# One unit boundary of a fused attention and gated-FFN kernel: scores and attention outputs gathered in one place each

## The chip, the cores and the metric

The kernel runs on one core of one Trainium2 chip. The metric is device time of one execution in microseconds (us). The kernel before took 254.5 us, the median of three runs (254.49, 254.50 and 255.01 us). Engines are called by the names of the profile: PE is the matrix engine and PEld its weight loads, DVE the vector engine, ACT the scalar engine, POOL the GpSimd engine, SP the engine that here only issues transfers.

## The reference, cut to what matters

Inputs are q, k, v of shape (4, 8, 768, 64), that is batch, heads, positions, head size, and four weight matrices. First comes an attention in which each position sees a band of its neighbours and one summary of each block of 32 positions:

```python
k_sum = k.reshape(B, H, nb, 32, D).max(axis=3)
v_sum = v.reshape(B, H, nb, 32, D).mean(axis=3)
scores_l = scale * q @ k.T            # kept only where |i - j| < 16
scores_s = scale * q @ k_sum.T + log(32)
a = softmax(concat[scores_l, scores_s])
x = a @ concat[v, v_sum]              # then (4*768, 512)
```

Then a gated feed-forward with a gated residual:

```python
ffn = (gelu(x @ w_gate) * (x @ w_val)) @ w_out
out = x + sigmoid(x @ w_res) * ffn
```

The model width is 512 (8 heads of 64), the inner width 1536, and there are 3072 rows of x.

## The kernel before, in words

The rows are cut into eight units of 384 positions (`TU`), two to a batch entry. A unit has three sub-blocks of 128 rows (`NSUB`), and its heads are handled as four pairs (`hp`). All matrix operands are bf16. The order of instructions on every engine is the order in which the code issues them (`tc.manual_schedule()`), so the order of the source lines is the order of each engine's queue. The framework adds the waits.

The work of a unit has two halves. In the first, for each of twelve columns of the inner width (`fo`), PE makes `g` and `vv` (line 451), ACT takes the Gelu of `g` (456), and DVE multiplies it by `vv` into `gvT` (457). In the second, the output half, PE makes the residual gate `r` (`res_step`, 492) and ACT its tanh into `th` (495); PE multiplies `gvT` by `w_out` into `f` (`ffn_step`, 502), twelve matmuls for each sub-block; and DVE combines `th`, `f` and x in two instructions (`end_step`, lines 508 and 511), after which SP sends 128 rows out.

Interleaved with the output half of unit u, the attention of unit u + 1 is made. Its steps are:

- **Scores.** PE multiplies keys by queries, 48 small matmuls (6 tiles x 2 heads x 4 pairs); ACT takes the exponential into `p_all`; DVE multiplies `p_all` by a mask. `s_step` does one pair (12 matmuls, one exponential of 768 columns or two of 384, one mask product). `s_all` (lines 343 to 373) does all four pairs packed into six PSUM banks of 512 columns: two tiles of the pool `ps_mm`, the two banks of `ps_s`, and the one tile each of `ps_t` and `ps_o`. It has five exponentials and six mask products of 512 columns.
- **Attention outputs.** PE multiplies `p_all` by the values into `ao`, 12 matmuls a pair; DVE divides by the sum, two instructions a pair (`av_end`, lines 429 and 431), into `xn`. `av_step` does one pair. `av_all` (375 to 398) does all four, with the `ao` tiles of pairs 0 and 1 in `ps_t` and `ps_o`, and of pairs 2 and 3 in `ps_s`.
- **Turning x.** The next first half needs x with its columns on the partitions (`xT`). From unit 2 on transfers do this (`xt_dma`). For unit 1 PE does it (`xt_step`, lines 433 to 438): three transposes into one PSUM tile and one copy out, on DVE unless ACT's copy is passed.

Three functions hold the three kinds of output half: `first_out` (unit 0's, which makes the attention of unit 1), `mid_out` (units 1 to 6) and `last_out`. `mid_out` uses `s_all` and `av_all`, one place each. `first_out` uses `s_step` and `av_step` in three or four places.

PSUM tiles are shared in turn. `ps_mm` has four banks, taken round by round by `g`, `vv`, `r`, `f` and by two of `s_all`'s tiles. `ps_t` and `ps_o` have one tile each, so whoever takes such a tile waits until the one before it was read. `w_out` arrives in three chunks of four `fo` (issued on line 213): chunk 1 serves `ffn_step(.., 0, 4)`, chunk 2 `(.., 4, 8)`, chunk 3 `(.., 8, 12)`.

Of the kernel before, what the change touches and what calls it, by code (L numbers as in the profile page):

```python
# [15 lines left out]
def kernel(  # L16
# [11 lines left out]
    nc = tc.nc  # L28
# [9 lines left out]
    FO = DFF // 128  # L38
# [4 lines left out]
    NSUB = TU // 128  # L43
# [16 lines left out]
    ps_o = ctx.enter_context(tc.tile_pool(name="ps_o", bufs=1, space=bass.MemoryType.PSUM))  # L60
    ps_t = ctx.enter_context(tc.tile_pool(name="ps_t", bufs=1, space=bass.MemoryType.PSUM))
# [77 lines left out]
    with tc.manual_schedule():  # L139
# [182 lines left out]
        def s_step(u, hp, st, banks=None, tiles=None):  # L322
            if tiles:
                s, banks = tiles, True
            elif banks:
                s = [p.tile([128, 512], F32, tag=tag, name="s") for p, tag in banks]
            else:
                s2 = ps_s.tile([128, 2, 512], F32, tag="s", name="s")
                s = [s2[:, hh] for hh in range(2)]
            s_mm(u, hp, [x[:, 0:TU] for x in s])  # L330
            P = p_all[:, :, hp * HT:(hp + 1) * HT]
            if banks:
                for hh in range(2):
                    nc.scalar.activation(P[:, hh].rearrange("p t q -> p (t q)"), s[hh][:, 0:TU], AF.Exp,
                                         scale=scale, bias=bias_t[:])
            else:
                nc.scalar.activation(P.rearrange("p a t q -> p a (t q)"), s2[:, :, 0:TU], AF.Exp,
                                     scale=scale, bias=bias_t[:])
            if u:
                nc.vector.tensor_mul(P, P, maskt.unsqueeze(1).unsqueeze(1).to_broadcast([128, 2, HT, QT]))  # L340
            st["P", hp] = P

        def s_all(u):
            b, half = u // 2, u % 2
            kw, qt = kW[b % 2], qT[b % 2]
            s2 = None
            for i in range(3):
                if i == 0:
                    s = [ps_mm.tile([128, 512], F32, tag="mm", name="s") for _ in range(2)]
                elif i == 1:  # L350
                    s2 = ps_s.tile([128, 2, 512], F32, tag="s", name="s")
                    s = [s2[:, hh] for hh in range(2)]
                else:
                    s = [p.tile([128, 512], F32, tag=tag, name="s") for p, tag in TO2]
                for j in range(8):
                    hp, t = divmod(8 * i + j, HT)
                    tt = half * HT + t
                    for hh in range(2):
                        ps = slice(hh * 64, hh * 64 + 64)
                        nc.tensor.matmul(s[hh][:, j * QT:(j + 1) * QT], kw[ps, tt, hp, :],  # L360
                                         qt[ps, tt // 2, hp, (tt % 2) * QT:(tt % 2 + 1) * QT],
                                         start=True, stop=True, skip_group_check=True)
                js = slice(8 * i, 8 * i + 8)
                m = maskt.unsqueeze(1).to_broadcast([128, 8, QT])
                for hh in range(1 if i == 1 else 2):
                    if i == 1:
                        nc.scalar.activation(p_all[:, :, js].rearrange("p a j q -> p a (j q)"), s2[:], AF.Exp,
                                             scale=scale, bias=bias_t[:])
                    else:
                        nc.scalar.activation(p_all[:, hh, js].rearrange("p j q -> p (j q)"), s[hh][:], AF.Exp,  # L370
                                             scale=scale, bias=bias_t[:])
                for hh in range(2):
                    nc.vector.tensor_mul(p_all[:, hh, js], p_all[:, hh, js], m)  # L373
# [27 lines left out]
        TO2 = ((ps_t, "t"), (ps_o, "ao"))  # L401

        def av_step(u, hp, st, pool=ps_o, tag="ao"):
            b, half = u // 2, u % 2
            P = st["P", hp]
            ao = pool.tile([128, NSUB, 2, D + 1], F32, tag=tag, name="ao")
            for sub in range(NSUB):
                for hh in range(2):
                    for e in range(2):
                        t = 2 * sub + e  # L410
                        nc.tensor.matmul(ao[64 * e:64 * e + 64, sub, hh, :], P[:, hh, t, :],
                                         vext[b % 2][:, half * HT + t, 2 * hp + hh, 0:D + 1],
                                         start=True, stop=True, skip_group_check=True)
            av_end(hp, st, ao)
# [12 lines left out]
        def av_end(hp, st, ao):  # L427
            rz = work.tile([128, NSUB, 2, 1], F32, tag="rz", name="rz")
            nc.vector.reciprocal(rz[:], ao[:, :, :, D:D + 1])  # L429
            xn = st["xn"][:, hp].rearrange("p s (h d) -> p s h d", d=D)  # L430
            nc.vector.tensor_mul(xn, ao[:, :, :, 0:D], rz.to_broadcast([128, NSUB, 2, D]))  # L431

        def xt_step(u, ko, st, pool, tag, copy=nc.vector.tensor_copy):
            xp = pool.tile([128, TU], BF16, tag=tag, name="xp")
            for sub in range(NSUB):
                nc.tensor.transpose(xp[:, sub * 128:(sub + 1) * 128],  # L436
                                    st["xn"][:, ko, sub, :], ident[:])
            copy(st["xT"][:, ko, :], xp[:])
# [5 lines left out]
        def new_unit():  # L444
            return {"xn": upool.tile([128, KO, NSUB, 128], BF16, tag="xn", name="xn"),
                    "xT": upool.tile([128, KO, TU], BF16, tag="xT", name="xT")}
# [12 lines left out]
        def mm_tile(name):  # L459
            return ps_mm.tile([128, 512], F32, tag="mm", name=name)  # L460
# [27 lines left out]
        def res_step(st, sub):  # L488
            ss = slice(sub * 128, (sub + 1) * 128)
            r = mm_tile("r")  # L490
            for ko in range(KO):
                nc.tensor.matmul(r[:], st["xT"][:, ko, ss], w_res[:, ko, :],  # L492
                                 start=(ko == 0), stop=(ko == KO - 1))
            st["th", sub] = work.tile([128, DM], F32, tag="th", name="th")
            nc.scalar.activation(st["th", sub][:], r[:], AF.Tanh, scale=0.5)  # L495

        def ffn_step(st, gvT, sub, lo, hi):
            ss = slice(sub * 128, (sub + 1) * 128)
            if lo == 0:
                st["f", sub] = mm_tile("f")  # L500
            for fo in range(lo, hi):
                nc.tensor.matmul(st["f", sub][:], gvT[:, fo, ss], w_out[:, fo, :],  # L502
                                 start=(fo == 0), stop=(fo == FO - 1), skip_group_check=True)
# [13 lines left out]
        def end_step(u, st, sub):  # L517
            end_part(u, st, sub, st["f", sub], slice(0, DM))
# [19 lines left out]
        tk, tq, ao = {}, {}, {}  # L538
# [11 lines left out]
        st = new_unit()  # L550
        gvT = upool.tile([128, FO, TU], BF16, tag="gvT", name="gvT")
# [91 lines left out]

        def first_out(u, st, gvT, nst):
            n = u + 1
            other = dict(pool=ps_t, tag="t")
            turn = dict(pool=ps_t, tag="t", copy=nc.scalar.copy)
            s_step(n, 0, nst)
            s_step(n, 1, nst, TO2)
            for sub in range(NSUB):  # L650
                res_step(st, sub)
            ffn_step(st, gvT, 0, 0, 4)
            av_step(n, 0, nst)
            av_step(n, 1, nst, **other)
            s_step(n, 2, nst)
            ffn_step(st, gvT, 1, 0, 4)
            ffn_step(st, gvT, 2, 0, 4)
            ffn_step(st, gvT, 0, 4, 8)
            xt_step(n, 0, nst, **turn)
            av_step(n, 2, nst)  # L660
            s_step(n, 3, nst)
            ffn_step(st, gvT, 1, 4, 8)
            ffn_step(st, gvT, 2, 4, 8)
            ffn_step(st, gvT, 0, 8, FO)
            xt_step(n, 1, nst, **turn)
            av_step(n, 3, nst)
            ffn_step(st, gvT, 1, 8, FO)
            xt_step(n, 2, nst, **turn)
            xt_step(n, 3, nst, ps_o, "ao")
            end_step(u, st, 0)  # L670
            ffn_step(st, gvT, 2, 8, FO)
            end_step(u, st, 1)
            end_step(u, st, 2)

        def mid_out(u, st, gvT, nst):
# [25 lines left out]
        for u in range(NU):  # L701
# [7 lines left out]
            if u:  # L709
                gvT = upool.tile([128, FO, TU], BF16, tag="gvT", name="gvT")  # L710
# [48 lines left out]
            else:  # L759
                nst = new_unit()  # L760
                (mid_out if u else first_out)(u, st, gvT, nst)
                st = nst
# [30 lines left out]
```

## Time and profile before

| what | value |
|---|---|
| median of three runs | 254.5 us |
| the profiled execution's own time | 255.01 us |
| its span from first to last instruction | 252.9 us |
| PE busy | 248.1 us, 98% of the span |
| PE weight loads busy | 139.5 us, 55% |
| DVE busy | 159.0 us, 63% |
| ACT busy | 127.9 us, 51% |
| POOL busy | 96.5 us, 38% |
| granted PE clock, mean | 0.998 |
| `f` matmuls, line 502 (128x512) | 276 records, 63.6 us |
| `r` matmuls, line 492 (128x512) | 96, 23.1 us |
| unit 0's output half on PE, first score matmul to the next unit's first `g` | 38.17 to 51.67 us |

The span is the time between the first and the last instruction of the program; the execution's own time, 2.1 us longer, takes in what lies around it. A matmul's record is longer than the time until the next one may start, since matmuls are pipelined; what a group of matmuls costs is therefore read from the start of the group to the start of the next group.

### The profile page before, as it was taken

The page shows a single profiled execution, that of the slowest core. Times are in us where ns is not written, and L with a number is a line of the kernel's source. Part 1 is how long each engine was busy: PE and PEld are TensorE (multiplying, and loading weights), DVE is VectorE, ACT ScalarE, POOL GpSimd, SP SyncE. Part 2 cuts the span into 40 slices and gives each one's busy share as a digit, 9 for nine tenths or more (in the row PEclk, how much of TensorE's full clock was granted, in tenths as well). Part 3 has the DMA queues.
Part 4 walks back from the last instruction along what each step waited for, and adds up shares of the span by engine and source line. Part 5 has one row for each costly group of instructions (what it writes and reads, how often), then busy time and mean ns, then how long its engine had stood idle before and what let it go on. Part 6 is the DMA issues. An engine that isn't in the chain of part 4 may idle for free.

```text
span 252.9 us, 5881 instructions
## 1 busy us (share of the span) xinstructions
PE 248.1 (98%) x2328; PEld 139.5 (55%) x2328; DVE 159.0 (63%) x376; ACT 127.9 (51%) x210; POOL 96.5 (38%) x128
## 2 busy tenths in 40 slices
PE   8999999999999999999999999999999999999994
PEld 2676565565654665446554665546554565456544
DVE  6995796398557544768557545758557545754424
ACT  8885458256582338254572338243572338243320
POOL 8885442360632881247332990247331000000000
PEclk9999999999999999999999999999999999999999
DMA  5999999999403999959903999769903600140003
GB/s 78 178 182 197 197 204 207 178 168 235 68 4 62 199 148 125 104 158 157 139 3 62 207 151 149 74 169 152 133 3 62 167 4 0 34 156 0 3 0 124
DMA packets 98106, 29.33 MB, mean 116 GB/s; under 512 B 83224, under 2 KB 94944, under 8 KB 97984
## 3 DMA queue, kind: packets, MB, share of 16 engines
q0 software_dynamic: 68352, 14.76, 67.0%
q1 hardware_dynamic: 29728, 14.21, 27.1%
q8 instruction: 18, 0.29, 0.5%
q14 instruction: 8, 0.07, 0.1%
HBM read 29.36 MB, written 6.29 MB: 141 GB/s over the span
## 4 chain that ended last, share of the span: by engine, by line
PE 93%; DVE 5%; issue 1%; DVEq 0%
PE g L451 25%; PE vv L451 24%; PE f L502 24%; PE r L492 8%; PE ao L390 2%; PE s L360 2%; PE vs L282 1%; PE tp L220 1%; PE ao L423 1%; PE vs L290 1%; PE s L317 1%; PE wp L534 1%; DVE ks L237 1%; DVE o L511 1%; PE xp L436 1%
## 5 line engine op out<-in xcount | busy, mean ns | idle before, releaser
L451 PE MATMUL g<-xT,w_gate 128*128 128x384 bf16 x380 | 78.0, 326 | 0.0
L451 PE MATMUL vv<-xT,w_val 128*128 128x384 bf16 x380 | 77.7, 326 | 0.0
L456 ACT ACTIVATE ge<-g 128x384 f32<-128x384 f32 x81 | 39.7, 490 | 61.0 <-DVE gvT L457 30.0
L457 DVE TENSOR_TENSOR gvT<-ge,vv 128x384 bf16<-128x384 f32 x81 | 44.3, 549 | 38.1 <-PE vv L451 34.0
L502 PE MATMUL f<-w_out,gvT 128*128 128x512 bf16 x276 | 63.6, 379 | 0.0
L451 PEld LDWEIGHTS <-w_gate 128*128 128x128 bf16 x384 | 37.1, 98 | 26.2 <-issue 1.4
L451 PEld LDWEIGHTS <-w_val 128*128 128x128 bf16 x384 | 37.6, 98 | 25.2 <-issue 0.5
L502 PEld LDWEIGHTS <-gvT 128*128 128x128 bf16 x276 | 26.2, 98 | 30.6
L107 POOL DMA_DIRECT2D vext<-in_v_dram x32 | 24.1, 767 | 15.2 <-DMA w_out<-in_moe_w_out_dram 5.6
L495 ACT ACTIVATE th<-r 128x512 f32<-128x512 f32 x24 | 13.6, 614 | 30.8 <-PE r L492 30.8
L508 DVE SCALAR_TENSOR_TENSOR th<-th,f 128x512 f32<-128x512 f32 (+2 forms) x26 | 16.6, 640 | 13.4 <-PE f L502 13.4
L492 PE MATMUL r<-w_res,xT 128*128 128x512 bf16 x96 | 23.1, 380 | 0.0
L302 POOL COPY vext<-vsum 32x1536 bf16<-32x1536 bf16 x12 | 17.2, 1463 | 11.8 <-DMA vsum<-vpart 11.6
L373 DVE TENSOR_TENSOR p_all<-p_all,maskt 128x512 bf16<-128x512 bf16 x36 | 14.2, 423 | 8.3 <-ACT p_all L370 4.5
L431 DVE TENSOR_TENSOR xn<-ao,rz 128x384 bf16<-128x384 f32 x32 | 17.8, 557 | 1.1
L511 DVE SCALAR_TENSOR_TENSOR o<-th,xn 128x512 f32<-128x512 f32 (+2 forms) x26 | 16.9, 651 | 0.9
L127 POOL DMA_DIRECT2D q_nat<-in_q_dram x18 | 15.8, 904 | 0.6 <-issue 0.5
L370 ACT ACTIVATE p_all<-s,bias_t 128x512 bf16<-128x512 f32 x24 | 15.2, 692 | 0.1
L237 DVE TENSOR_REDUCE ks<-kW 128x24 bf16<-128x768 bf16 x16 | 15.1, 941 | 0.0
L486 DVE TENSOR_TENSOR gvT<-ge,vv 128x384 bf16<-128x384 f32 x14 | 7.8, 554 | 10.4 <-PE vv L451 9.8
L492 PEld LDWEIGHTS <-xT 128*128 128x128 bf16 x96 | 8.8, 98 | 9.9
L429 DVE RECIPROCAL rz<-ao 128x6 f32<-128x6 f32 x32 | 6.0, 189 | 11.4 <-PE ao L390 7.0
(100 smaller groups left out, 209.0 us busy)
## 6 DMA issues: line engine op xcount, KB each, us to landing
out_dram<-o SPq DMA_DIRECT2D x23, 256.0 KB, 2.3
vext<-in_v_dram POOLq DMA_DIRECT2D x32, 96.0 KB, 6.2
q_nat<-in_q_dram POOLq DMA_DIRECT2D x18, 128.0 KB, 6.1
w_gate<-in_moe_w_gate_dram POOLq DMA_DIRECT2D x6, 256.0 KB, 9.1
w_val<-in_moe_w_val_dram POOLq DMA_DIRECT2D x6, 256.0 KB, 9.7
w_out<-in_moe_w_out_dram POOLq DMA_DIRECT2D x3, 512.0 KB, 14.3
k_nat<-in_k_dram POOLq DMA_DIRECT2D x16, 96.0 KB, 5.8
vext<-vext SPq DMA_DIRECT2D x6, 144.0 KB, 4.6
```

The lines of the kernel that those rows point to most:

```text
L107: nc.gpsimd.dma_start(out=vext[b % 2][0:QT, :, h, 0:D], in_=v[b, h].rearrange("(t p) d -> p t d", p=QT))
L127: nc.gpsimd.dma_start(out=q_nat[:, c].rearrange("p (h d) -> p h d", d=D), in_=q[b, :, c * 128:(c + 1) * 128, :].rearrange("h p d -> p h d"))
L237: nc.vector.tensor_reduce(out=ks.rearrange("d (t n) -> d t n", n=2), in_=kw[:, :, 0:QT].rearrange("d t (n w) -> d t n w", w=BLK), axis=myb ...
L302: eng.tensor_copy(vext[b % 2][96:128, lo:hi, :, 0:D], src)
L431: nc.vector.tensor_mul(xn, ao[:, :, :, 0:D], rz.to_broadcast([128, NSUB, 2, D]))
L451: nc.tensor.matmul(ps[:, 0:TU], w[:, ko, fo * 128:(fo + 1) * 128], st["xT"][:, ko, :], start=(ko == 0), stop=(ko == KO - 1), skip_group_ch ...
L456: nc.scalar.activation(ge[:], g[:, 0:TU], AF.Gelu)
L457: nc.vector.tensor_mul(gvT[:, fo, :], ge[:], vv[:, 0:TU])
L492: nc.tensor.matmul(r[:], st["xT"][:, ko, ss], w_res[:, ko, :], start=(ko == 0), stop=(ko == KO - 1))
L502: nc.tensor.matmul(st["f", sub][:], gvT[:, fo, ss], w_out[:, fo, :], start=(fo == 0), stop=(fo == FO - 1), skip_group_check=True)
L508: nc.vector.scalar_tensor_tensor(th[:, cs], th[:, cs], 1.0, f[:, 0:n], ALU.add, ALU.mult)
L511: nc.vector.scalar_tensor_tensor(o.rearrange("p (k d) -> p k d", d=128), th[:, cs].rearrange("p (k d) -> p k d", d=128), 0.5, x, ALU.mult, ...
```

## The change

Only `first_out` is changed. Its scores now come from `s_all` and its attention outputs from `av_all`, one place each, as in `mid_out`. The `res_step` and `ffn_step` calls are put in another order: two `res_step`, then the first eight `fo` of sub-blocks 0 and 1, then the attention outputs, then the rest of sub-blocks 0 and 1, each followed by its `end_step`, then sub-block 2. The four `xt_step` stand together, between the first third and the rest of sub-block 2's `ffn_step`. They take `ps_t`, `ps_o`, `ps_t`, `ps_o` in turn, with the copies on ACT, DVE, ACT, DVE; before, three copies were on ACT and the last on DVE. In `av_all` nothing is changed: for unit 1 it issues no `xt_dma`.

```diff
         def first_out(u, st, gvT, nst):
             n = u + 1
-            other = dict(pool=ps_t, tag="t")
-            turn = dict(pool=ps_t, tag="t", copy=nc.scalar.copy)
-            s_step(n, 0, nst)
-            s_step(n, 1, nst, TO2)
-            for sub in range(NSUB):
-                res_step(st, sub)
-            ffn_step(st, gvT, 0, 0, 4)
-            av_step(n, 0, nst)
-            av_step(n, 1, nst, **other)
-            s_step(n, 2, nst)
-            ffn_step(st, gvT, 1, 0, 4)
+            s_all(n)
+            res_step(st, 0)
+            res_step(st, 1)
+            for lo in (0, 4):
+                for sub in range(2):
+                    ffn_step(st, gvT, sub, lo, lo + 4)
+            av_all(n, nst)
+            for sub in range(2):
+                ffn_step(st, gvT, sub, 8, FO)
+                end_step(u, st, sub)
+            res_step(st, 2)
             ffn_step(st, gvT, 2, 0, 4)
-            ffn_step(st, gvT, 0, 4, 8)
-            xt_step(n, 0, nst, **turn)
-            av_step(n, 2, nst)
-            s_step(n, 3, nst)
-            ffn_step(st, gvT, 1, 4, 8)
-            ffn_step(st, gvT, 2, 4, 8)
-            ffn_step(st, gvT, 0, 8, FO)
-            xt_step(n, 1, nst, **turn)
-            av_step(n, 3, nst)
-            ffn_step(st, gvT, 1, 8, FO)
-            xt_step(n, 2, nst, **turn)
+            xt_step(n, 0, nst, ps_t, "t", nc.scalar.copy)
+            xt_step(n, 1, nst, ps_o, "ao")
+            xt_step(n, 2, nst, ps_t, "t", nc.scalar.copy)
             xt_step(n, 3, nst, ps_o, "ao")
-            end_step(u, st, 0)
-            ffn_step(st, gvT, 2, 8, FO)
-            end_step(u, st, 1)
+            ffn_step(st, gvT, 2, 4, FO)
             end_step(u, st, 2)
```

## The prediction, made before the changed kernel ran

> **What bounds the kernel now.** I read the page's engine shares first, then the chain of work that ended last, then the waits of PE alone, and then the timeline of the one stretch that the change touches.
>
> ```profile
> PE 248.1 (98%) x2328; PEld 139.5 (55%) x2328; DVE 159.0 (63%) x376; ACT 127.9 (51%) x210; POOL 96.5 (38%) x128
> ...
> PE 93%; DVE 5%; issue 1%; DVEq 0%
> ```
>
> PE is busy 98% of the span and carries 93% of the chain. Its list of waits has one matmul wait in the whole run (1.2 us, at the first instruction), and for its weight loads, beside that same one, none over 0.8 us. So PE is the bound everywhere, and any time added to or taken from PE in unit 0's output half moves everything behind it, up to the end. In that stretch the PE timeline is:
>
> ```profile
> 38.17 0.52 PE L317 MATMUL s<-qT,kW 64*128 64x64 bf16 x24
> 38.63 2.76 PE L492 MATMUL r<-w_res,xT 128*128 128x512 bf16 x12
> 41.23 1.03 PE L502 MATMUL f<-w_out,gvT 128*128 128x512 bf16 x4
> 42.19 0.57 PE L411 MATMUL ao<-vext,p_all 128*64 128x65 bf16 x24
> 42.69 0.35 PE L317 MATMUL s<-qT,kW 64*128 64x64 bf16 x12
> 42.97 2.76 PE L502 MATMUL f<-w_out,gvT 128*128 128x512 bf16 x12
> 45.57 0.33 PE L436 MATMUL xp<-ident,xn 128*128 128x128 bf16 x3
> 45.83 0.38 PE L411 MATMUL ao<-vext,p_all 128*64 128x65 bf16 x12
> ...
> 50.47 0.50 PE L436 MATMUL xp<-ident,xn 128*128 128x128 bf16 x6
> 50.81 1.03 PE L502 MATMUL f<-w_out,gvT 128*128 128x512 bf16 x4
> 51.67 0.81 PE L451 MATMUL g<-xT,w_gate 128*128 128x384 bf16 x4
> ```
>
> The reader is to take start-to-start times: 12 of `f` cost 45.57 - 42.97 = 2.60 us, 0.216 each. Groups follow without a hole; the stretch is 51.67 - 38.17 = 13.50 us.
>
> For the packed forms, which this stretch doesn't have yet, unit 1's output half is the row. From the PE and the DVE timelines there:
>
> ```profile
> 69.82 0.87 PE L360 MATMUL s<-qT,kW 64*128 64x64 bf16 x48
> 70.62 1.90 PE L492 MATMUL r<-w_res,xT 128*128 128x512 bf16 x8
> 72.36 2.75 PE L502 MATMUL f<-w_out,gvT 128*128 128x512 bf16 x12
> 75.04 0.95 PE L390 MATMUL ao<-vext,p_all 128*64 128x65 bf16 x48
> ...
> 75.47 0.20 DVE L429 RECIPROCAL rz<-ao 128x6 f32<-128x6 f32 x1 [1.16 <-PE ao L390]
> ...
> 78.25 0.68 DVE L508 SCALAR_TENSOR_TENSOR th<-th,f 128x512 f32<-128x512 f32 x1
> ...
> 79.57 0.68 DVE L508 SCALAR_TENSOR_TENSOR th<-th,f 128x512 f32<-128x512 f32 x1
> ```
>
> **Part 1: packing, on PE.** The matmuls are the same in number: 48 scores, 48 outputs, 12 transposes, 12 `r`, 36 `f`. What goes is edges between kinds. Scores: before 0.46 + 0.28 + 0.28 = 1.02 us, packed 70.62 - 69.82 = 0.80; gain 0.22. Outputs: before 0.50 + 0.31 + 0.31 = 1.12, and 0.10 ahead of the first group (41.23 to 42.19 is 0.96 for four `f` of 0.216); packed 75.93 - 75.04 = 0.89, and 0.09 ahead (72.36 to 75.04 is 2.68 for twelve); gain 0.24. Transposes: before 0.26 + 0.27 + 0.34 = 0.87; twelve together at 0.34 / 6 each 0.68; gain 0.19. Sum 0.65 us, if nothing waits.
>
> [...] The rows here have 0.80 / 48 = 17 ns, and the measurement decides.
>
> **Part 2: the front of the new order.** PE's times in the changed kernel: `s_all` 38.17, `r` 38.97, `f` 40.71 (unit 1's 1.74 for eight `r`), sixteen `f` 16 x 0.216 + 0.09 = 3.55, outputs at 44.26. What must be ready for that? ACT can start its exponentials at 39.43 as now (the table load ends then). In unit 1 the exponentials start at 70.42 and the last mask product ends at 74.31, so 3.89 later: 43.32 here, 0.94 before the outputs. The exponentials free two `ps_mm` banks for `f` at about 40.1 and 40.7, against 40.71 and 41.57. Nothing waits. If this cover were gone, the outputs would start later by what is missing, one for one.
>
> The `w_out` chunks are new near-misses. Their issues on POOL and the three times to landing:
>
> ```profile
> 26.03 0.74 POOL L213 DMA_DIRECT2D w_out<-in_moe_w_out_dram x1 [0.65 <-DMA w_gate<-in_moe_w_gate_dram]
> ...
> 27.93 1.52 POOL L213 DMA_DIRECT2D w_out<-in_moe_w_out_dram x2 [1.16 <-DMA w_val<-in_moe_w_val_dram]
> ```
> ```profile
> DMA to landing us min/median/max: 13.5/14.3/16.0
> ```
>
> In the order of issue they take 13.5, 14.3 and 16.0 us and land at 39.5, 42.2 and 44.8. Before, `f` needed them at 41.23, 44.70 and 48.15. Now it needs them at 40.71, 40.71 + 8 x 0.216 = 42.44, and after the outputs at 45.15. The margins shrink to 1.2, 0.2 and 0.4 us. I take no wait, as their own landings say; if chunk 2 took 16.0 us like its neighbour, it would land at 43.9 and cost 1.5.
>
> **Part 3: a new wait, at the end.** From the outputs' start A = 44.26, PE does outputs 0.89, eight `f` 1.73, four `r` 0.86, four `f` 0.86, and stands at the transposes 4.34 later, at 48.60. The four `xt_step` share two banks: the third waits for the first's copy (ACT), the fourth for the second's copy, which is on DVE. In the program that copy stands behind four `av_end` and two `end_step`. DVE from A, by unit 1's rows: first reciprocal 75.47 - 75.04 = 0.43; four `av_end` 78.25 - 75.47 = 2.78; two `end_step` at 79.57 - 78.25 = 1.32 each, 2.64; then the copy, 0.36 (its row before: 51.01 0.36). It ends at A + 6.21 = 50.47. From there to PE's restart no row shows this very wait: not below 0, since the bank is being read; ACT to DVE is 0.03 (the exponential of 39.43 ends at 40.33, the mask product starts at 40.36); and the weight load of 42.19 came 0.33 after the mask product (41.30 + 0.56) that is named as its releaser, under other matmuls. I take 0.05, near the 0.03. The last three transposes then start at 50.52, where without a wait they would start at 48.60 + 9 x 0.057 = 49.11: **1.41 us lost**. The third `xt_step` is inside that: its ACT copy follows the transposes by 0.37 and takes 0.48 (rows at 45.57 and 45.94), 49.45, and ACT is idle there.
>
> Behind PE's wait stand eight `f` (1.73) and all of unit 1. `g` starts at 50.52 + 0.17 + 1.73 = 52.42, against 51.67: **+0.75** (-0.65 + 1.41, rounded).
>
> **What is hidden.** DVE's last copy of `xT` is done near 51.1, before `g`. `end_step` 0 and 1 now finish some 4 us earlier, so that DVE is freer when unit 1 begins; before, PE already ran through unit 1 with no wait (its waits list names none there), so nothing is won. POOL's loads and SP's transfers keep their order; two of three output transfers leave earlier, and nothing waits for them. `k_sb` lands at 30.0 + 18.7 = 48.7, for transposes at 53.1.
>
> **Sum.** Profiled execution: 255.01 + 0.75 = 255.76. It was the longest of the three runs; on the median, 254.5 + 0.75, I forecast **255.3 us**.
>
> **Rivals.** (a) *The wait doesn't form, and it is faster.* Place: the second `xt_step`'s copy on DVE. It decides once DVE's chain from A is shorter by over 0.75 of its 6.21 us, or PE is as much longer on the way. With all of it gone: 254.5 - 0.65 = 253.9. For it speaks only that the chain is long; against it, that two `av_end` take 1.40 in unit 0 (42.62 to 44.02) and 1.39 in unit 1, and that `end_step` takes 1.32 in both. Chance 0.06.
> (b) *The loss is absorbed later*: a wait of PE's behind unit 0 that doesn't move with it, of 0.75 or more. Time 254.5. PE's waits list speaks against it. Chance 0.05.
> (c) *A `w_out` chunk comes late.* Chunk 2 has 0.2 us; beyond that each tenth adds a tenth. Half a microsecond late: 255.3 + 0.5 = 255.8, at the bound 256.8. For it: the margin is smaller than the 0.5 us by which the three executions differ. Against: the landings of this trace. Chunk 3 late costs nothing up to 1.4 us, since PE waits for DVE anyhow. Chance 0.11.
> (d) *The clock falls in the hole.* At the end of the span PE's last matmul ends at 249.6, and the granted clock by windows is 1.00 up to 251, 0.98 from 251 to 252, and 0.50 after: it fell some 2.4 us after the last matmul. The new holes are 0.55 and 0.85 us, with transposes between. By that row there is no fall. No row prices one; half the clock for as long as the holes last, 1.4 us, would lose another 0.7, so 256.0 or more. Chance 0.03.
> [...]
>
> **How the numbers follow.** The forecast's own range is 254.9 to 255.7: the release between 0 and 0.33, the packing gain 0.2 to either side, and chunk 2 a little late; chance 0.75. A measurement of this kernel can tell about 0.2%, 0.5 us. Faster takes (a), 0.06; same takes (b) and 0.07 of the forecast's lower edge, 0.12; slower the rest, 0.82. The range 254.8 to 256.0 leaves out (a), (b), (d) and the upper part of (c), some 0.18.
>
> **What would show it.** In the changed profile: scores 48 in about 0.80, then `r` at +0.80; outputs near 44.3 after sixteen `f`; nine transposes, a hole that a DVE `xT` copy ends, the last three near 50.5, and `g` near 52.4; DVE back to back from the first reciprocal to that copy. A hole ahead of the fifth `f` of a sub-block means (c). No hole ahead of the last transposes, or a `g` of unit 1 before 51.7, would make the prediction wrong.

## The result, and the profile after

The changed kernel takes 255.62 us (median of four runs, 255.53 to 255.88), the kernel before 254.50 us in the same comparison. The ratio is 1.0042, with a 95% interval of 1.0024 to 1.0059: slower by 0.6 to 1.5 us. The forecast was 255.3, the range 254.8 to 256.0. The profiled execution took 255.56 us, its span is 253.5 us.

First the shares, from the page: the engine line, and the shares of the chain that ended last by engine.

```profile
PE 246.7 (97%) x2328; PEld 139.2 (55%) x2328; DVE 158.9 (63%) x379; ACT 127.3 (50%) x209; POOL 96.2 (38%) x128
...
PE 90%; DVE 7%; issue 1%; DMA 1%; DVEq 0%
```

PE has fewer busy microseconds than before, 246.7 against 248.1, and the kernel is slower: a matrix engine that is busy less is not a gain when it stands still instead. DVE's share of the chain has grown from 5% to 7%. Where, the PE timeline of unit 0's output half tells (columns: start, duration, engine, line, what; in brackets the idle time before it and who ended it):

```profile
38.21 0.87 PE L360 MATMUL s<-qT,kW 64*128 64x64 bf16 x48
39.02 1.90 PE L492 MATMUL r<-w_res,xT 128*128 128x512 bf16 x8
40.76 3.62 PE L502 MATMUL f<-w_out,gvT 128*128 128x512 bf16 x16
44.30 0.95 PE L390 MATMUL ao<-vext,p_all 128*64 128x65 bf16 x48
...
48.65 0.50 PE L436 MATMUL xp<-ident,xn 128*128 128x128 bf16 x6
49.54 0.33 PE L436 MATMUL xp<-ident,xn 128*128 128x128 bf16 x3 [0.40 <-DVE th L508]
50.57 0.33 PE L436 MATMUL xp<-ident,xn 128*128 128x128 bf16 x3 [0.70 <-DVE xT L438]
50.73 1.89 PE L502 MATMUL f<-w_out,gvT 128*128 128x512 bf16 x8
52.46 0.81 PE L451 MATMUL g<-xT,w_gate 128*128 128x384 bf16 x4
```

Two holes now stand in a stretch that had none, both among the transposes. From the first score matmul to the next unit's first `g` it is 52.46 - 38.21 = 14.25 us, against 13.50 before. The transposes and their holes take 50.73 - 48.65 = 2.08 us; the run with a tile each, below, shows them at 0.67 without holes, so 1.41 us are lost. (The two bracketed idle times add to 1.10 only, because a matmul's record reaches some 0.16 us beyond the start of what follows it without a wait, as in 47.78 + 1.03 = 48.81 against 48.65; starts are the better ruler.)

What ended the second hole is in the DVE timeline:

```profile
44.73 0.20 DVE L429 RECIPROCAL rz<-ao 128x6 f32<-128x6 f32 x1 [1.38 <-PE ao L390]
...
47.52 0.68 DVE L508 SCALAR_TENSOR_TENSOR th<-th,f 128x512 f32<-128x512 f32 x1
48.23 0.69 DVE L511 SCALAR_TENSOR_TENSOR o<-th,xn 128x512 f32<-128x512 f32 x1
48.84 0.68 DVE L508 SCALAR_TENSOR_TENSOR th<-th,f 128x512 f32<-128x512 f32 x1
49.56 0.69 DVE L511 SCALAR_TENSOR_TENSOR o<-th,xn 128x512 f32<-128x512 f32 x1
50.17 0.35 DVE L438 COPY xT<-xp 128x384 bf16<-128x384 bf16 x1
50.93 0.36 DVE L438 COPY xT<-xp 128x384 bf16<-128x384 bf16 x1 [0.42 <-PE xp L436]
```

From 44.73 to 50.52 DVE has no idle time in brackets: it is a queue, worked off without a break. The second turning step's transposes end at 49.15 in their record (48.65 + 0.50); their copy starts at 50.17 because two `end_step` stand ahead of it. It ends at 50.52, and PE's last three transposes, which need that bank, start at 50.57.

The chain that ended last, in order of time, goes the same way (start, duration, what): from the outputs on PE into DVE's queue, and back to PE through the copy.

```profile
44.37 0.34 PE ao L390 x12
...
48.84 0.69 DVE th L508
49.53 0.02 issue
49.56 0.69 DVE o L511
50.25 0.28 DVE xT L438
50.52 0.04 issue
50.57 0.33 PE xp L436 x3
50.90 1.73 PE f L502 x8
```

Before, the chain in this stretch lay on PE alone. The shift stays to the end: the packed scores of unit 1's output half start at 70.61 (69.82 before), those of unit 2's at 98.46 (97.67), +0.79 both times, and the last `f` group at 247.36 (246.79), +0.57; where the difference of 0.22 lies is told under "Hidden work".

### The profile page after: what moved, and what is told of

Same layout as the page of the kernel before. It is cut to its first block, busy times and chain, and to the rows that moved or that the text cites. A ratio compares the mean times of both kernels' runs of the same rounds, so it can differ in the third digit from the quotient of the medians.

```text
span 253.5 us, 5885 instructions
## 1 busy us (share of the span) xinstructions
PE 246.7 (97%) x2328; PEld 139.2 (55%) x2328; DVE 158.9 (63%) x379; ACT 127.3 (50%) x209; POOL 96.2 (38%) x128
## 4 chain that ended last, share of the span: by engine, by line
PE 90%; DVE 7%; issue 1%; DMA 1%; DVEq 0%
PE g L451 25%; PE vv L451 24%; PE f L502 22%; PE r L492 8%; PE s L360 2%; PE ao L390 2%; DVE th L508 1%; PE vs L282 1%; DVE o L511 1%; PE tp L220 1%; PE ao L423 1%; DMA xT<-xn 1%; PE vs L290 1%; DVE ks L237 1%; PE wp L534 1%
## 5 line engine op out<-in xcount | busy, mean ns | idle before, releaser
L451 PE MATMUL g<-xT,w_gate 128*128 128x384 bf16 x380 | 78.0, 326 | 0.0
L451 PE MATMUL vv<-xT,w_val 128*128 128x384 bf16 x380 | 77.8, 326 | 0.0
L451 PEld LDWEIGHTS <-w_gate 128*128 128x128 bf16 x384 | 37.1, 98 | 26.2 <-issue 1.4
L451 PEld LDWEIGHTS <-w_val 128*128 128x128 bf16 x384 | 37.6, 98 | 24.9 <-issue 0.3
L508 DVE SCALAR_TENSOR_TENSOR th<-th,f 128x512 f32<-128x512 f32 (+2 forms) x26 | 16.7, 641 | 14.9 <-PE f L502 14.9
L373 DVE TENSOR_TENSOR p_all<-p_all,maskt 128x512 bf16<-128x512 bf16 x42 | 16.6, 423 | 9.7 <-ACT p_all L370 5.2
L370 ACT ACTIVATE p_all<-s,bias_t 128x512 bf16<-128x512 f32 x28 | 17.8, 692 | 0.1
L121 POOL DMA_DIRECT2D k_nat<-in_k_dram x16 | 12.0, 798 | 0.6 <-issue 0.6
## 6 DMA issues: line engine op xcount, KB each, us to landing
out_dram<-o SPq DMA_DIRECT2D x23, 256.0 KB, 2.3
w_gate<-in_moe_w_gate_dram POOLq DMA_DIRECT2D x6, 256.0 KB, 8.7
w_val<-in_moe_w_val_dram POOLq DMA_DIRECT2D x6, 256.0 KB, 9.0
w_out<-in_moe_w_out_dram POOLq DMA_DIRECT2D x3, 512.0 KB, 14.1
```

Of the source, the lines that this page charges most:

```text
L451: nc.tensor.matmul(ps[:, 0:TU], w[:, ko, fo * 128:(fo + 1) * 128], st["xT"][:, ko, :], start=(ko == 0), stop=(ko == KO - 1), skip_group_ch ...
L508: nc.vector.scalar_tensor_tensor(th[:, cs], th[:, cs], 1.0, f[:, 0:n], ALU.add, ALU.mult)
```

## The experiments

The theory was the prediction's: one place each for scores, outputs and transposes gives PE 0.65 us back, and the shared bank of the fourth `xt_step` makes it wait 1.41 us for a copy that stands in DVE's queue. The rivals: the new order itself costs (another wait would come up in place of this one), or there is a second loss of some 0.35 us that the span doesn't show, since the first medians lie 1.1 us apart and not 0.75. All diffs are against the changed kernel; "stretch" is from the first score matmul to unit 1's first `g` in the PE timeline.

### The changed kernel once more

No edit.

> The changed kernel itself, unaltered, timed in five rounds for a finer ratio. My theory (packing gains 0.65 us, the fourth turning step then waits 1.41 us for a copy on the vector engine) says +0.75 us against the kernel before, 255.25. The rival (a second loss of some 0.35 us that the profile's span does not show) says +1.1, as the first medians had it.

Measured: 255.31 us against 254.60, ratio 1.0037 (1.0017 to 1.0057); the stretch is 52.31 - 38.06 = 14.25 us, as in the first profile. By the medians it is +0.71, by the ratio +0.9. The interval holds the theory's +0.75 and the rival's +1.1, so the times alone don't decide; the stretch does not move by a hundredth.

### A bank each, but not a tile each

```diff
-            xt_step(n, 2, nst, ps_t, "t", nc.scalar.copy)
-            xt_step(n, 3, nst, ps_o, "ao")
+            x2 = ps_s.tile([128, 2, 1024], BF16, tag="s", name="xp")
+            xt_step(n, 2, nst, None, None, nc.scalar.copy, x2[:, 0, 0:TU])
+            xt_step(n, 3, nst, None, None, xp=x2[:, 1, 0:TU])
```

> The changed kernel with a bank of its own for each of the four turning steps (steps 3 and 4 in the two banks of ps_s), so that no turning step waits for a copy; order and engine of every copy stay. My theory says that the whole hole of 1.41 us goes: the first g of unit 1 near 51.05 on the profile's clock, 0.65 us less than the kernel before, 253.85. Rival 1 (the loss is in the new order itself, or comes back as a wait of g for the late copies) says that the time stays near that of the changed kernel, +0.75 to +1.1. Rival 2 (an extra loss of 0.35 elsewhere) says 0.3 under the kernel before, 254.2.

Measured: 254.97 us, ratio 1.0013 (1.0004 to 1.0023). This is a miss: not under the kernel before, but over it. The PE timeline (line numbers are one higher in this kernel):

```profile
48.54 0.67 PE L437 MATMUL xp<-ident,xn 128*128 128x128 bf16 x9
49.82 0.33 PE L437 MATMUL xp<-ident,xn 128*128 128x128 bf16 x3 [0.61 <-ACT xT L439]
49.98 1.89 PE L503 MATMUL f<-w_out,gvT 128*128 128x512 bf16 x8
51.71 0.81 PE L452 MATMUL g<-xT,w_gate 128*128 128x384 bf16 x4
```

The third step no longer waits: nine transposes stand together. The fourth does, for another copy: ACT's, out of the other bank. ACT's two copies, the second out of the first bank, end at 48.91 + 0.86 = 49.77 and the fourth step starts at 49.82, so in this run the two banks of one tile were one thing to the waits that the framework adds, and my edit had put a new wait in the place of the old. The stretch is 51.71 - 38.10 = 13.61 us, +0.11 against before. The run still tells one thing. In the changed kernel's profile the first hole (49.54) is put down to `DVE th L508`. Here DVE's `th` runs at the same place and the third step doesn't wait, so DVE's `th` wasn't its releaser. First `th` in this run, on DVE, then ACT's copy in the changed kernel:

```profile
48.74 0.68 DVE L509 SCALAR_TENSOR_TENSOR th<-th,f 128x512 f32<-128x512 f32 x1
```
```profile
49.01 0.48 ACT L438 COPY xT<-xp 128x384 bf16<-128x384 bf16 x1 [0.43 <-PE xp L436]
```

What this edit took away was the shared bank `ps_t`, that is, the wait for ACT's copy. In the changed kernel that copy runs from 49.01 to 49.49, and the third step starts at 49.54, the same 0.05 behind it as the fourth is behind DVE's copy.

### One `end_step` moved behind the copies

```diff
-            for sub in range(2):
-                ffn_step(st, gvT, sub, 8, FO)
-                end_step(u, st, sub)
+            ffn_step(st, gvT, 0, 8, FO)
+            end_step(u, st, 0)
+            ffn_step(st, gvT, 1, 8, FO)
...
             xt_step(n, 3, nst, ps_o, "ao")
+            end_step(u, st, 1)
```

> The changed kernel with the end_step of sub-block 1 issued behind the four turning steps: the vector engine's copy stands behind one end_step instead of two. My theory says that this copy then ends near 49.4, ahead of the scalar engine's copy that the third turning step waits for, so that a hole of about 0.4 to 0.55 us is left: g near 51.6, 0.1 under the kernel before, 254.4. The rival (the loss isn't the queue on the vector engine) says no change against the changed kernel, 255.3 to 255.6.

Measured: 254.60 us, ratio 0.9996 (0.9987 to 1.0004). The stretch is 51.50 - 38.11 = 13.39 us, -0.11 against before; the theory said -0.1. One line of the PE timeline and one of the DVE timeline:

```profile
49.44 0.49 PE L436 MATMUL xp<-ident,xn 128*128 128x128 bf16 x6 [0.40 <-DVE xT L438]
```
```profile
49.08 0.36 DVE L438 COPY xT<-xp 128x384 bf16<-128x384 bf16 x1 [0.26 <-PE xp L436]
```

The copy on DVE now runs at 49.08, and one hole of 0.40 is left, ahead of the third step, which starts 0.05 us after ACT's copy ends (48.91 + 0.48). The profile names DVE's copy, which ends just as the step starts (49.08 + 0.36), but the third step takes the bank that ACT's copy reads. Moving two DVE instructions behind the copies takes 0.86 us out of PE's stretch (14.25 to 13.39), with PE's own instructions and their order untouched. What is left over the 12.83 us of the run with a tile each, 0.56, is the wait for ACT's copy: the 1.41 us are two waits, of which DVE's queue alone makes 0.86.

### The second copy on ACT

```diff
-            xt_step(n, 1, nst, ps_o, "ao")
+            xt_step(n, 1, nst, ps_o, "ao", nc.scalar.copy)
```

> The changed kernel with the second turning step's copy on the scalar engine too. My theory says: copies back to back on the scalar engine, 49.0 to 49.5 and to 50.0, so that the fourth step starts near 50.0 instead of 50.57; 0.55 us won, g near 51.9, +0.2 against the kernel before, 254.7. The rival says no change against the changed kernel, 255.3 to 255.6.

Measured: 254.71 us, ratio 1.0004 (0.9996 to 1.0013). The stretch is 51.77 - 38.16 = 13.61 us: the time gained, 0.64 us against the changed kernel's 14.25, is a little more than the 0.55 expected, since ACT's copies follow each other faster than their durations (three in 1.37 us, where one alone takes 0.48 in the changed kernel). The rival's "no change" is out. The lines, from PE and from ACT:

```profile
49.50 0.71 PE L436 MATMUL xp<-ident,xn 128*128 128x128 bf16 x6 [0.40 <-DVE th L508]
```
```profile
48.97 1.37 ACT L438 COPY xT<-xp 128x384 bf16<-128x384 bf16 x3 [0.43 <-PE xp L436]
```

### A tile each

```diff
-            xt_step(n, 2, nst, ps_t, "t", nc.scalar.copy)
-            xt_step(n, 3, nst, ps_o, "ao")
+            xt_step(n, 2, nst, ps_s, "s", nc.scalar.copy)
+            xt_step(n, 3, nst, *mm)
```

> The changed kernel with four separate tiles for the four turning steps: ps_t, ps_o, ps_s and the next tile of ps_mm. In the run before with steps 3 and 4 in two banks of one tile, step 4 waited 0.61 us for the scalar engine's copy out of the other bank, since the two banks are one tile to the waits. My theory: here nothing waits, the twelve transposes stand together in 0.68 us, and the stretch from the first score matmul to unit 1's first g is 13.50 - 0.65 = 12.85 us; time 0.65 under the kernel before, 253.9 to 254.0. The rival (the packing gives back less than it should, or g then waits for the copies that stand behind the two end_step): stretch 13.3 to 13.5, time within 0.2 of the kernel before.

Measured: 254.06 us against 254.82, ratio 0.9974 (0.9964 to 0.9985). Two lines that name another tile turn the loss into a gain of 0.66 us by the ratio, 0.76 by the medians. The PE timeline:

```profile
38.12 0.88 PE L360 MATMUL s<-qT,kW 64*128 64x64 bf16 x48
...
48.55 0.83 PE L436 MATMUL xp<-ident,xn 128*128 128x128 bf16 x12
49.22 1.89 PE L502 MATMUL f<-w_out,gvT 128*128 128x512 bf16 x8
50.95 0.81 PE L451 MATMUL g<-xT,w_gate 128*128 128x384 bf16 x4
```

Twelve transposes in one group, 0.67 us, no hole; the stretch is 50.95 - 38.12 = 12.83 us, where the theory had 12.85. The DVE timeline of the same run shows that DVE is as late as ever:

```profile
48.75 0.68 DVE L508 SCALAR_TENSOR_TENSOR th<-th,f 128x512 f32<-128x512 f32 x1
49.46 0.69 DVE L511 SCALAR_TENSOR_TENSOR o<-th,xn 128x512 f32<-128x512 f32 x1
50.07 0.61 DVE L438 COPY xT<-xp 128x384 bf16<-128x384 bf16 x2
```

The two copies end at 50.68, and `g` starts at 50.95. The same queue, just as long, costs nothing now: what hurt was not that the copies were late but that PE needed their banks before it could go on to the eight `f`, which have nothing to do with them.

### The queue made longer

```diff
             ffn_step(st, gvT, 2, 0, 4)
+            for _ in range(2):
+                nc.vector.memset(warm[:], 0.0)
             xt_step(n, 0, nst, ps_t, "t", nc.scalar.copy)
```

> The changed kernel with two memsets of a tile that is not used any more (128x256 words each, 0.27 us in the trace of the kernel before) on the vector engine between the second end_step and the turning steps' copies. My theory: they stand in the queue ahead of the copy that the fourth turning step waits for, so the hole and the time grow by their whole 0.54 us: g at +1.3 us against the kernel before, 255.9. The rival (the vector engine's queue doesn't set the end of the hole): no change against the changed kernel, 255.3.

Measured: 256.20 us against 254.82, ratio 1.0051 (1.0036 to 1.0067). The PE timeline has the same first hole and a longer second:

```profile
49.63 0.33 PE L436 MATMUL xp<-ident,xn 128*128 128x128 bf16 x3 [0.40 <-DVE th L508]
51.26 0.33 PE L436 MATMUL xp<-ident,xn 128*128 128x128 bf16 x3 [1.31 <-DVE xT L438]
```

The hole grows from 0.70 to 1.31, the stretch from 14.25 to 53.16 - 38.30 = 14.86: +0.61, where 0.54 was expected (the copy starts 0.58 us after the first memset in this trace). Work that nobody needs, on an engine that is busy two thirds of the time, goes one for one into the time of the kernel, through this one copy.

## Why the prediction was right

**What bounds the kernel** held: PE's starts carried the loss of unit 0 through all units.

**Part 1, packing.** Scores 39.02 - 38.21 = 0.81 (0.80 said), outputs 45.18 - 44.30 = 0.88 (0.89), twelve transposes 0.67 once nothing waits (0.68). The sum of 0.65 is shown by the run with a tile each: 0.67 in the stretch, 0.66 in the time by the ratio. The score matmuls again stand 17 ns apart on average (0.81 / 48).

**Part 2, the front.** The last mask product ends at 43.35 (43.32 said), the outputs start at 44.30. Chunk 2 of `w_out` landed at 27.9 + 14.1 = 42.0 and was needed at 40.76 + 8 x 0.216 = 42.49, a margin of 0.5 instead of 0.2; no `f` waited for a chunk in any of the runs. Rival (c), a late chunk, didn't come.

**Part 3, the wait.** DVE's copy ended 6.22 us after the outputs began (50.52 - 44.30), where 6.21 was worked out, and PE restarted 0.05 us later, as taken; that term was a choice between 0 and 0.33, so that it fits to the hundredth is in part luck. The loss of 1.41 us and the +0.75 for the stretch came out to the hundredth. The step is shown, not only argued, by four edits: one that shortens the queue (one `end_step` behind the copies, -0.86), one that leaves the queue for another engine (the second copy on ACT, -0.64), one that lengthens it (two memsets, +0.61), and one that leaves it alone and takes the shared tiles away (a tile each, -1.42). Two readings on the way were off, without weight in the sum. The prediction looked for nine transposes and one hole, but by its own row ACT's copy ends at 49.45, after the 48.94 at which the third step could start (48.60 + 6 x 0.057); there are six, three and three, with two holes, as rival (d) counts them. And DVE's last copy ends at 51.29, where the prediction had 51.1; its own terms give 51.25 (50.52 + 0.37 + 0.36).

**Hidden work.** Rival (a), no wait, and rival (b), a loss that is absorbed later, are out: the wait formed, and every later unit's packed scores and the last group still start 0.57 to 0.79 us later than before. The 0.22 between these two figures lies at the starts of units 5 to 7. There PE's fourth `g` matmul needs the last quarter of `xT`, which a transfer brings; in the profile after, the chain that ended last goes through one such transfer:

```profile
194.75 2.32 DMA xT<-xn
```

It ends at 197.07, and PE goes on at 197.11. Beyond the 0.49 us of the three `vv` matmuls ahead of it, that `g` starts 0.17, 0.07 and 0.18 us late in units 5, 6 and 7 before, and 0, 0.20 and 0 after: 0.42 against 0.20. In the profile before, the transfers issued at 194.00 and 222.05 land 2.3 us later, 0.06 and 0.05 us ahead of that `g` in units 6 and 7. PE's lists of waits before and after name none of them, and they differ between executions: the list of the run with two memsets has one of this kind, `PE g L451 <- DMA xT<-xn`, of 0.2 us.

**The size** is where the prediction is least certain. The first medians differ by 1.1 us, the second comparison's by 0.71, and both intervals hold +0.75. The larger ratio of the second comparison, +0.9, comes from one of its eleven executions, 258.26 us; the other ten have a mean of 255.30 against 254.64 before, +0.67. A loss outside the span is not there: in that comparison the spans have medians of 253.4 and 252.7 us, and the time is 1.9 us longer than the span for both kernels. I found nothing in the traces for a second loss inside it: in the run with a tile each the time fell by 0.66 by the ratio and the stretch by 0.67. In the run with two banks the time is +0.3 for a stretch of +0.11, with an interval of +0.1 to +0.6. Whether the changed kernel loses another 0.1 or 0.2 us outside the stretch, beyond the small waits at the unit starts, stays open.

**One row was read too far**: rival (d) took from the end of the span that the clock falls some 2.4 us after the last matmul. In the profile after, it had not fallen 3.3 us after it (last matmul done at 250.2, granted clock 1.00 to the end at 253.5). No single delay fits both, and what sets the moment of the fall no run here shows. Through the holes among the transposes in the profile after (0.40 and 0.70 us) and in the run with two memsets (0.40 and 1.31 us) the granted clock was 1.00.

## What to carry to other kernels

Work that is gathered into one place on the bound engine saves its edges, some 0.2 us a kind here, but it also gathers what used to be spread: banks that were free by the time they were needed again are now asked for back to back, and each step waits for whoever reads the bank that it takes over (0.40 and 0.70 us in the changed kernel). Before steps are put together, follow each PSUM tile to the instruction that frees it, on the engine where that stands, and count everything queued ahead of it; an engine that is idle a third of the time can still be the one that is late. And where the profile names a releaser, look at which instruction the wait can mean: the name that ended at the right moment is not always the one that was waited for.

## What the runs showed of the hardware

A wait across engines costs little here: PE started 0.05 us after the end of the copy it waited for, from DVE (50.52 to 50.57) and from ACT (49.49 to 49.54) alike. The records of copies on one engine overlap: one ACT copy takes 0.48 us (the changed kernel) and three together 1.37 (the run with the second copy on ACT); one on DVE takes 0.35 (the changed kernel) and two together 0.61 (the run with a tile each).
